# Linear attention and gated experts on one core: weights staged in the maxima's tiles, epsilon on ScalarE, factors transposed straight out of PSUM, another order

## The chip, the cores and the metric

The kernel runs on one core of a Trainium2 chip, in float32 throughout. The metric is device time in microseconds (us). Its engines are TensorE (PE, with its weight loads as PEld), VectorE (DVE), ScalarE (ACT), GpSimd (POOL) and SyncE (SP, which issues the transfers). TensorE writes into PSUM, of which the kernel uses eight banks of 128 partitions x 512 elements; the other engines take the results from there into SBUF.

## What is computed

```python
# q, k, v: [8, 8, 576, 64] (batch, heads, seq, head_dim); w_phi: [64, 128]
def phi(x):
    proj = x @ w_phi
    proj = proj - max(abs(proj), axis=-1)
    return concat([exp(proj), exp(-proj)], axis=-1)
q_p, k_p = phi(q), phi(k)
kv, z = k_p^T v, sum(k_p, axis=seq)
x = (q_p @ kv) / (q_p @ z + 1e-6)            # -> [8, 576, 512]
logits = x @ w_gate                          # 4 experts, the best 2 of each row
w = softmax over the two chosen logits
for e in range(4):
    q, k, v = x @ wq[e], x @ wk[e], x @ wv[e]        # 64 wide
    a = softmax(causal(q k^T / 8)), its sum + 1e-9
    out += w[e] * (a @ v) @ wo[e]
```

## The kernel before

The work is cut into 32 pairs of heads (4 for each of the 8 batches) for the linear attention, and into 16 halves (2 experts each, 2 for each batch) for the experts. Float32 products with weights are made of three products of a high and a low part (`mm`, L302 to L310).

A pair p goes through these steps. `stream_k` (L502) projects the keys; `center` (L544) takes the largest magnitude of each row on VectorE (L550) and subtracts it (L564); ScalarE takes both exponentials (L526, L528, recorded as L321). `stream_kv` (L575) multiplies the key features with v (L591) and with ones (L607), and brings the result into the layout of a stationary operand: for p < KVD = 4 by three transposes on TensorE (L618), for the others by a VectorE transpose (L626) and a way through DRAM, four stores and one load. `stream_q` (L637) projects the queries (L646, recorded as L500), `phi_q` (L661) takes the maximum over partitions on GpSimd (L666), subtracts on VectorE (L668) and takes the exponentials. `stream_n` (L675) computes the denominators (L693) and the numerators (L704).

`fractions` (L709) turns a row of sums into factors laid out as the numerators are. It is called for each pair and, from `sums` (L973), for each half, 48 times in all. VectorE transposes the sums in 32x32 blocks out of PSUM into a tile `wide` (L715); ScalarE picks the 4 x 9 columns that count and writes them back into the same PSUM bank (L720); VectorE adds epsilon (L722) and takes the reciprocal (L723), for the experts also times the gate (L726); one copy spreads the 18 values to 576 columns, each 32 times, into `wide` (L730, on ScalarE or VectorE; recorded as L319 or L331), the bank is released, and VectorE transposes `wide` into `xf` or `rb` (L733). `divide` (L736) multiplies the numerators with `xf` and splits the quotient x into a high and a low part.

A batch then takes `stream_b` (L755): q and k projections (`proj_t`), scores (L825), their evacuation, the mask on GpSimd (L929), `maxima` (L932): the largest of the key blocks in the tile `top` (L939, L942), the maximum over partitions on GpSimd into the tile `max` (L946), subtraction (L950) and exponentials; `sums` (L988) and `attend` (L997, L1017) make y, `evac_y` scales it and splits it, `project_out` (L1040) multiplies both halves' y with wo into eight products (4 tiles of 128 rows, 2 parts of 256 and 320 columns), `evac_o` copies them into one of two tiles `ot`, and `store` writes a tile to DRAM.

The weights arrive in pieces (`split_w`, `split_piece`, L421 to L442): two transfers of 64 partitions into a stage, a rounded copy (high part), and a subtraction (low part). Pieces have up to 576 columns; qk and wo are staged in `ot0`, vg in `ot1`. `load` (L340) issues all transfers from SyncE's queue.

The order of all instructions is made by a planner (`Plan`, L113 to L268) when the kernel is built. Each stream yields a `Step` with its engine or engines, what it needs and what must be done before. The planner keeps a clock per engine and takes, of the steps that could start within WINDOW of the earliest, the one with the lowest rank. A rank is the pair's or batch's number plus the constants POS, POS1, BOFF, SLOPE and MOVE; HOT is taken off for evacuations, OTHER is added for a step on TensorE with another array tiling than the last (128x128 for L310 and L618, 64x128 for L500 and L825, 128x32 for L591, L607, L693, L704, L911, L988 and L1017). FLEX is a handicap for copies that VectorE or ScalarE can do. The engines then follow that order (`in_order`). While nothing else is there at the start, `keep_warm` (L466) issues matmuls on a constant tile.

```python
        st = Step(copies(S), [pk], hot=True)                          # L728
        yield st
        copy(st.eng, S, X.rearrange("p (t i) -> p t i", i=32), both.unsqueeze(2).to_broadcast([128, 18, 32]), [key], [pk])
        plan.release('c', (pk, ps))
        yield Step('DVE', [key], pred=free, hot=True)
        dve(S, wk, [key], 1.1).transpose(out, X)                      # L733
```

Of the kernel before, what the change touches and what calls it, by code (L numbers as in the profile page):

```python
# [21 lines left out]
NJ = 5  # L22
# [18 lines left out]
HOT = 8.54  # L41
SLOPE = (-34.57, 3.93, 4.47, 8.35, -11.91)
UB = 4
SADD = 0
FLEX = (281, -146)
QB = 1
EKB = 2
# [3 lines left out]
WINDOW = 45.0  # L51
SWITCH = 0.0
# [3 lines left out]
ZEROS = 31.82  # L56

MOVE = {
# [29 lines left out]

POS = {'p0': 5.23, 'p1': -38.0, 'v0': 13.08, 'gate': -8.29, 's0': 6.44, 's1': -1.9, 'm0': 9.53, 'm1': 13.64, 't0': -7.83, 't1': 10.17, 'out': 21.57}
NPAIRS = B * NP  # L90
HEAD = 2.4
ADDS = (0, 2)
KVD = 4
RATE = 2.18
TRATE = 2.37
CHANGE = (150.0, 190.0)
PORT = 350.0
OTHER = 6.05
LDW = 109.0
PSUM_TILES = (("c", 8, 512),)  # L100


def moved(x, i):

# [1030 lines left out]
```

## Time and profile before

| | |
|---|---|
| median of 3 runs | 631.66 us (630.19 to 631.81) |
| the profiled execution, its own time | 634.48 us |
| its span, first to last instruction | 632.7 us |
| TensorE matmuls, busy | 615.0 us, 8442 instructions |
| VectorE, busy | 559.3 us, 1176 |
| ScalarE, busy | 444.5 us, 1052 |
| GpSimd, busy | 250.3 us, 167 |
| granted TensorE clock, mean | 0.994 |

The profile is of one execution; times in it are counted from the span's start. Busy times are unions of an engine's instructions. Matmuls overlap in the pipeline, so that the time of one (some 300 ns) is longer than the distance to the next; what a run of them costs is seen in the chain of waits, which follows the work that ended last back from the end, at each step to what released it or to the instruction before it. The kernel's lines L310, L314, L319, L321, L331 and L500 are helpers that several steps share, so that the names of the tiles (out<-in) tell which step it is. A granted clock of 1.00 is 2.4 GHz; the lower level is 1.2 GHz.

### The profile page before, as it was taken

The page shows a single profiled execution, that of the slowest core. Times are in us where ns is not written, and L with a number is a line of the kernel's source. Part 1 is how long each engine was busy: PE and PEld are TensorE (multiplying, and loading weights), DVE is VectorE, ACT ScalarE, POOL GpSimd, SP SyncE. Part 2 cuts the span into 40 slices and gives each one's busy share as a digit, 9 for nine tenths or more (in the row PEclk, how much of TensorE's full clock was granted, in tenths as well). Part 3 has the DMA queues.
Part 4 walks back from the last instruction along what each step waited for, and adds up shares of the span by engine and source line. Part 5 has one row for each costly group of instructions (what it writes and reads, how often), then busy time and mean ns, then how long its engine had stood idle before and what let it go on. Part 6 is the DMA issues. An engine that isn't in the chain of part 4 may idle for free.

```text
span 632.7 us, 20442 instructions
## 1 busy us (share of the span) xinstructions
PE 615.0 (97%) x8442; PEld 479.7 (76%) x8442; DVE 559.3 (88%) x1176; ACT 444.5 (70%) x1052; POOL 250.3 (40%) x167
## 2 busy tenths in 40 slices
PE   8899999999999999999999999999999999999996
PEld 7675688668796778868886878867798578877985
DVE  6599999999998999999999999899967999776782
ACT  3499688568686798676776886676857678664653
POOL 0474626282244544225165506074017254510520
PEclk9899999999999999999999999999999999999998
DMA  6553412341233421234213422142421211110021
GB/s 169 165 153 108 129 48 73 97 116 37 70 115 98 115 66 60 90 102 117 70 51 108 131 89 67 35 142 84 126 94 32 79 48 26 61 43 3 1 76 76
DMA packets 43691, 53.29 MB, mean 84 GB/s; under 512 B 22480, under 2 KB 26576, under 8 KB 43600
## 3 DMA queue, kind: packets, MB, share of 16 engines
q1 hardware_dynamic: 43600, 52.00, 28.5%
q8 instruction: 66, 1.08, 0.7%
q14 instruction: 25, 0.20, 0.1%
HBM read 37.04 MB, written 14.94 MB: 82 GB/s over the span
## 4 chain that ended last, share of the span: by engine, by line
PE 65%; DVE 17%; ACT 8%; issue 3%; POOL 3%; DMA 2%; SPq 1%; DVEq 0%; ACTq 0%; POOLq 0%
PE ps_c L310 27%; PE ps_c L500 8%; PE ps_c L591 7%; PE ps_c L704 6%; PE ps_c L825 5%; PE ps_c L1017 5%; PE ps_c L693 3%; PE ps_c L988 2%; DVE top L942 2%; DVE s L950 2%; DMA ot<-in_wts_dram 2%; ACT u L319 2%; PE ps_c L607 1%; POOL max L946 1%; DVE zs L537 1%
## 5 line engine op out<-in xcount | busy, mean ns | idle before, releaser
L666 POOL PARTITION_ALL_REDUCE mx<-u x64 | 142.8, 2276 | 149.3 <-ACT u L319 146.2
L310 PE MATMUL ps_c<-xh,qk 128*128 128x320 f32 (+1 forms) x512 | 105.7, 297 | 0.0
L929 POOL TENSOR_SCALAR_AFFINE_SELECT s<-s 128x256 f32<-128x256 f32 (+1 forms) x80 | 46.1, 608 | 140.0 <-ACT s L319 123.2
L946 POOL PARTITION_ALL_REDUCE max<-top x16 | 61.8, 3864 | 66.9 <-DVE top L942 53.1
L310 PEld LDWEIGHTS ps_c<-xh,qk 128*128 128x128 f32 x512 | 82.6, 188 | 2.2 <-ACT u L319 0.9
L321 ACT ACTIVATE ek<-ek 128x1152 f32<-128x1152 f32 x64 | 74.9, 1170 | 8.0 <-DVE ek L564 7.2
L310 PE MATMUL ps_c<-xl,qk 128*128 128x256 f32 (+1 forms) x256 | 75.5, 295 | 1.9 <-DVE xl L314 1.9
L591 PE MATMUL ps_c<-ek,v_in 128*32 128x256 f32 x1280 | 75.4, 381 | 0.8 <-ACT ek L321 0.4
L950 DVE TENSOR_TENSOR s<-s,max 128x1152 f32<-128x1152 f32 (+4 forms) x80 | 71.4, 918 | 5.2 <-POOL max L946 5.1
L591 PEld LDWEIGHTS ps_c<-ek,v_in 128*32 128x32 f32 x1280 | 39.8, 110 | 29.6 <-issue 1.6
L321 ACT ACTIVATE s<-s 128x1152 f32<-128x1152 f32 (+4 forms) x80 | 56.5, 743 | 4.8 <-DVE s L950 4.5
L310 PE MATMUL ps_c<-vg,xh 128*128 128x260 f32 (+1 forms) x320 | 59.6, 287 | 0.0
L550 DVE TENSOR_REDUCE pmax<-ps_c 128x4 f32<-128x512 f32 (+1 forms) x96 | 49.4, 539 | 8.6 <-PE ps_c L500 7.2
L319 ACT COPY s<-ps_c 128x512 f32<-128x512 f32 (+4 forms) x141 | 49.3, 448 | 10.8 <-PE ps_c L825 10.8
L668 DVE TENSOR_TENSOR u<-u,mx 128x576 f32<-128x576 f32 x64 | 56.4, 896 | 0.5 <-POOL mx L666 0.5
L310 PE MATMUL ps_c<-yh,wo 128*128 128x256 f32 (+1 forms) x256 | 54.2, 307 | 2.4 <-ACT yh L319 2.4
L321 ACT ACTIVATE mx<-u 128x576 f32<-128x576 f32 x64 | 43.9, 687 | 12.5 <-DVE u L668 12.3
L537 DVE TENSOR_TENSOR zs<-zs,ek 128x512 f32<-128x512 f32 x56 | 51.5, 920 | 0.6
L319 ACT COPY u<-ps_c 128x256 f32<-128x256 f32 (+1 forms) x122 | 41.3, 408 | 14.1 <-PE ps_c L500 14.0
L500 PE MATMUL ps_c<-q_in,wf 64*128 64x320 f32 (+1 forms) x256 | 45.6, 440 | 5.5 <-DMA q_in<-in_qt_dram 2.5
L564 DVE TENSOR_TENSOR ek<-ps_c,pmax 128x512 f32<-128x512 f32 (+1 forms) x96 | 50.0, 536 | 0.0
L310 PEld LDWEIGHTS ps_c<-xl,qk 128*128 128x128 f32 x256 | 48.1, 188 | 2.3 <-DVE xl L314 2.3
(124 smaller groups left out, 1426.8 us busy)
## 6 DMA issues: line engine op xcount, KB each, us to landing
v_in<-in_v_dram SPq DMA_DIRECT2D x32, 320.0 KB, 3.0
q_in<-in_qt_dram SPq DMA_DIRECT2D x64, 144.0 KB, 2.9
out_dram<-ot SPq DMA_DIRECT2D x32, 288.0 KB, 2.1
kvd<-kvt SPq DMA_DIRECT2D x112, 48.0 KB, 1.9
kv<-kvd SPq DMA_DIRECT2D x28, 192.0 KB, 2.4
k_in<-in_kt_dram SPq DMA_DIRECT2D x32, 144.0 KB, 2.8
k_in<-in_kt_dram SPq DMA_DIRECT2D x32, 128.0 KB, 2.7
ot<-in_wts_dram SPq DMA_DIRECT2D x10, 144.0 KB, 3.2
```

Of the source, the lines that this page charges most:

```text
L310: nc.tensor.matmul(o, a, b, start=start, stop=stop, skip_group_check=True)
L319: nc.scalar.copy(o, i)
L321: nc.scalar.activation(o, i, func, **kw)
L500: nc.tensor.matmul(o, a, b, start=True, stop=True, skip_group_check=True)
L537: dve(512, ['zs'], ekk, 1.11, True).tensor_tensor(out=zs, in0=zs if a > 1 else x[:, :, :, 0], in1=x[:, :, :, a], op=ALU.add)
L550: dve(n * 128, [mk], [pk]).tensor_reduce(out=m[:, us], in_=src, axis=AX.X, op=ALU.max, apply_absolute_value=True)
L564: dve(n * 128, [e1k], [pk, mk]).tensor_tensor(out=ek2[p % EKB][:, 1, us, :], in0=src, in1=m[:, us].unsqueeze(2).to_broadcast([128, n, 128] ...
L591: nc.tensor.matmul(o[g, 0:2], v_in[:, 4 * h + t if t < 4 else 8 + h, k:64:2], ek[:, :, u_, :].rearrange("p c (w f) -> p c w f", w=4), star ...
L666: nc.gpsimd.partition_all_reduce(M, U, 128, bass_isa.ReduceOp.absmax)
L668: dve(S, [uk], [mk], port=True).tensor_tensor(out=U, in0=U, in1=M, op=ALU.subtract)
L946: nc.gpsimd.partition_all_reduce(big.rearrange("p e s -> p (e s)"), top.rearrange("p e s -> p (e s)"), 128, bass_isa.ReduceOp.max)
L950: dve(2 * (S - 128 * j), [('d', x, j)], [('max', z)], 1.11, True).tensor_tensor(out=block(s_, j, None, rows(j)), in0=block(s_, j, None, ro ...
```

## The change

- `fractions`: ScalarE's small copies add epsilon as the bias of an activation, the VectorE addition is gone. The spreading copy is gone: VectorE's second transpose reads the 18 values in PSUM with a step of zero, and the bank is released behind it.
- Weights: pieces of up to 1152 columns, staged in `top` and `max` in place of `ot` (qk in both, vg in `top`, wo in `max`, the last two behind all of qk). The first `maxima` waits for vg and wo. Their ranks are constants of their own: 7.17, 21.48 and 24.58.
- The q loads of the first two pairs are issued from ScalarE's queue.
- `project_out`: in the last batch (LAST = 7) the eight products are started when the first half's y is there, one tile's two at once and the others behind `attend` of the second half; each keeps its bank and is finished when the second half's y comes. In other batches a product waits for its own columns of y only.
- KVD is 6: pairs 4 and 5 too go through TensorE's transposes.
- `row` shares the memory of `ge`. KADD, KPOOL and PSUB are switches that, as set (3, 0, 0), leave `key_sum`, the sums of z and `phi_q` as they were.
- The planner's constants: OTHER 6.05 to 12.77, SWITCH 0 to 22, WINDOW 45 to 52, HOT 8.54 to 16.28, FLEX (281, -146) to (447, -293), all of POS, POS1, BOFF, SLOPE and MOVE, and its estimates for a transfer.

```diff
-HOT = 8.54
-SLOPE = (-34.57, 3.93, 4.47, 8.35, -11.91)
+HOT = 16.28
+SLOPE = (-37.28, -27.25, 9.68, 3.86, -6.2)
...
-FLEX = (281, -146)
+LAST = 7
+KADD = 3
+KPOOL = 0
+FLEX = (447, -293)
+PSUB = 0
...
-WINDOW = 45.0
-SWITCH = 0.0
+WINDOW = 52.0
+SWITCH = 22.0
...
-BOFF = (-6.43, -0.31, 4.51, 3.42, -4.56, -1.55, 18.35, 7.14)
+BOFF = (-2.11, 8.18, 6.82, 2.05, 1.07, 6.82, 22.72, -5.5)
...
-KVD = 4
+KVD = 6
...
-OTHER = 6.05
+OTHER = 12.77
...
-    def load(o, i, w, r=()):
-        plan.transfer(o.free_size() * o.partition_size() / 90.0, 475 if o.partition_size() == 128 else 650, [w], list(r))
-        nc.sync.dma_start(o, i)
+    def load(o, i, w, r=(), eng='SP'):
+        n = o.partition_size()
+        plan.transfer(o.free_size() * n / (55.0 if n == 128 else 45.0), 400 if n == 128 else 560, [w], list(r), eng)
+        (nc.scalar if eng == 'ACT' else nc.sync).dma_start(o, i)
...
-        for k, c0 in enumerate(range(0, n, S)):
-            pieces.append((name, c0, min(n, c0 + S), stage[k % len(stage)], src))
+        for k, c0 in enumerate(range(0, n, 2 * S)):
+            pieces.append((name, c0, min(n, c0 + 2 * S), *stage[k], src))
...
-        key, m = st.tensor.name, c1 - c0
-        yield Step('SP', pred=has('w', 1 if name == 'wo' else 0))
-        load(st[0:64, 0:m], src[0:128:2, c0:c1], (key, 0))
+        m = c1 - c0
+        yield Step('SP', pred=has('w', 0 if name == 'qk' else 1))
+        load(st[0:64, 0:m], src[0:128:2, c0:c1], key)
...
-    w_qk = split_w("qk", WQK, [ot[0]], wts[:, WP:c_vg])
-    w_vg = split_w("vg", WVG, [ot[1]], wts[:, c_vg:c_vg + WVG])
-    w_wo = split_w("wo", WO, [ot[0]], wts[:, c_vg + WVG:])
+    stages = [(t[0].rearrange("p e s -> p (e s)"), (n, 0)) for t, n in ((tops, "top"), (maxs, "max"))]
+    w_qk = split_w("qk", WQK, stages, wts[:, WP:c_vg])
+    w_vg = split_w("vg", WVG, stages, wts[:, c_vg:c_vg + WVG])
+    w_wo = split_w("wo", WO, stages[1:], wts[:, c_vg + WVG:])
...
-            yield Step('SP', pred=has('proj_q', p - IB) if p >= IB else None), of_pair('lq', p)
+            eng = 'ACT' if p < IB else 'SP'
+            yield Step(eng, pred=has('proj_q', p - IB) if p >= IB else None), of_pair('lq', p)
...
+                load(q_in[p % IB][64 * h:64 * h + 64, :], qt[p][:, S * h:S * h + S], (f'q_in{p % IB}', h), (), eng)
...
-                act(9, b3[w, :, src], X[r, 0:S // 2:32], [pk], [key])
+                act(9, b3[w, :, src], X[r, 0:S // 2:32], [pk], [key], bias=eps)
         yield Step('DVE', [pk], hot=True)
-        dve(18, [pk], []).tensor_scalar(out=both, in0=both, scalar1=eps, scalar2=None, op0=ALU.add)
         dve(18, [pk], [], 5.0).reciprocal(both, both)
...
-        st = Step(copies(S), [pk], hot=True)
-        yield st
-        copy(st.eng, S, X.rearrange("p (t i) -> p t i", i=32), both.unsqueeze(2).to_broadcast([128, 18, 32]), [key], [pk])
+        yield Step('DVE', [pk], pred=free, hot=True)
+        dve(S, wk, [pk], 1.1).transpose(out.rearrange("p (t i) -> p t i", i=32), both.unsqueeze(2).to_broadcast([128, 18, 32]))
         plan.release('c', (pk, ps))
-        yield Step('DVE', [key], pred=free, hot=True)
-        dve(S, wk, [key], 1.1).transpose(out, X)
...
-        free = lambda: ('m', n, 0) in done and (n < TB or ('max', n - TB) in done)
+        free = lambda: ('m', n, 0) in done and (('max', n - TB) in done if n >= TB else ('w', 2) in done and ('w', 3) in done)
...
-        if g == 1:
+        if g == (b < LAST):
...
-        wwo = wsp["wo"]
         for t in range(4):
-            for s0, s1 in PARTS:
-                yk = [('y' + x, g, s0) for x in "hl" for g in range(2)]
-                pk, ps = yield Step('PE', yk, 'c', lambda: ('w', 3) in done and has_y(2 * b) and has_y(2 * b + 1)), of_batch('out', b) + SLOPE[4] * t / 4
-                n = 0
-                for g in range(2):
-                    wc = slice(512 * g + 128 * t, 512 * g + 128 * t + 128)
-                    for y_, w_ in ((0, 0), (0, 1), (1, 0)):
-                        mm(ps[:, 0:s1 - s0], wwo[w_][:, wc], ys[g][y_][:, s0:s1], n == 0, n == 5, s1 - s0, pk,
-                           yk + [('wo', w_)])
-                        n += 1
-                plan.spawn(evac_o(b, t, s0, s1, pk, ps), of_batch('out', b))
+            for i, (s0, s1) in enumerate(PARTS):
+                if b < LAST:
+                    yield from out_unit(b, t, s0, s1)
+                else:
+                    plan.spawn(out_unit(b, t, s0, s1), of_batch('out', b) + SLOPE[4] * (2 * t + i) / 8)
             plan.spawn(store(b, t), of_batch('out', b))
         done.add(('o', b))
+
+    def out_unit(b, t, s0, s1):
+        wwo = wsp["wo"]
+        n = 0
+        for g in range(2):
+            yk = [('y' + x, g, s0) for x in "hl"]
+            if not g:
+                ks = yk if b >= LAST else [('y' + x, h, s0) for x in "hl" for h in range(2)]
+                pk, ps = yield Step('PE', ks, 'c', lambda: ('w', 3) in done and ('y', 2 * b, s0) in done and (('av', 2 * b + 1) in done or t < 1 if b >= LAST else ('y', 2 * b + 1, s0) in done)), of_batch('out', b) + SLOPE[4] * t / 4
+            elif b >= LAST:
+                yield Step('PE', yk, pred=lambda: ('y', 2 * b + 1, s0) in done), of_batch('fin', b)
+            wc = slice(512 * g + 128 * t, 512 * g + 128 * t + 128)
+            for y_, w_ in ((0, 0), (0, 1), (1, 0)):
+                mm(ps[:, 0:s1 - s0], wwo[w_][:, wc], ys[g][y_][:, s0:s1], n == 0, n == 5, s1 - s0, pk, yk + [('wo', w_)])
+                n += 1
+        plan.spawn(evac_o(b, t, s0, s1, pk, ps), of_batch('out', b))
...
-                     (weights(w_qk, ('w', 1)), 1.5), (weights(w_vg, ('w', 2)), 2.5),
-                     (weights(w_wo, ('w', 3)), 3.5), (stream_kv(), 0), (stream_n(), 0), (stream_s(), 0), (stream_t(), 0)):
+                     (weights(w_qk, ('w', 1)), POS1['wq']), (weights(w_vg, ('w', 2)), POS1['wv']),
+                     (weights(w_wo, ('w', 3)), POS1['wo']), (stream_kv(), 0), (stream_n(), 0), (stream_s(), 0), (stream_t(), 0)):
```

## Rows read from the trace of the kernel before

**Rows 1.** The page's first part: busy us (share of the span) x instructions

```profile
PE 615.0 (97%) x8442; PEld 479.7 (76%) x8442; DVE 559.3 (88%) x1176; ACT 444.5 (70%) x1052; POOL 250.3 (40%) x167
```

**Rows 2.** Busy time by stretch: us, busy (x) per engine, PEclk, DMA share, GB/s

```profile
0.00:5.20 5.20, 3.15 (x30) 2.98 (x30) 2.70 (x27) 0.00 (x0) 0.79 (x7) 1.00 0.38 98
...
19.50:36.00 16.50, 16.48 (x245) 12.06 (x249) 12.11 (x23) 10.40 (x20) 11.07 (x5) 0.90 0.47 132
...
50.00:550.00 500.00, 494.00 (x6779) 381.32 (x6776) 468.87 (x958) 369.64 (x884) 215.15 (x139) 1.00 0.29 83
...
621.00:632.70 11.70, 8.01 (x45) 7.59 (x45) 0.92 (x2) 3.62 (x9) 0.00 (x0) 0.82 0.26 101
```

**Rows 3.** TensorE's waits: line and what ended them, us, times, longest

```profile
PE ps_c L500 <- DMA q_in<-in_qt_dram: 2.5, 1, 2.5
PE ps_c L310 <- ACT yh L319: 2.4, 1, 2.4
PE ps_c L500 <- ACT s L319: 2.0, 2, 1.1
```

**Rows 4.** The chain of waits, its pieces: start us, us, what

```profile
86.09 6.54 PE ps_c L310 x48
92.63 2.08 PE ps_c L704 x32
...
95.68 1.76 PE ps_c L825 x24
97.44 2.30 PE ps_c L591 x40
...
201.92 0.71 PE ps_c L1017 x20
202.62 1.94 PE ps_c L704 x32
204.56 0.97 PE ps_c L693 x16
205.54 2.16 PE ps_c L591 x40
```

**Rows 5.** The timeline of the start: start us, us, engine, line, out<-in, [idle before]

```profile
14.05 2.38 SPq L342 DMA_DIRECT2D q_in<-in_qt_dram  x4
...
29.07 0.55 PE L618 MATMUL ps_c<-ident,kvt 128*128 128x128 f32 x3
```

**Rows 6.** First and last starts of the split of wo and of `top`

```profile
L314 DVE TENSOR_TENSOR wo<-ot,wo x2: 582/660/739, 43.4 to 50.3; 128x576 fp32r<-128x576 f32 x1, 128x448 fp32r<-128x448 f32 x1
...
L319 ACT COPY top<-s x10: 390/406/429, 87.8 to 586.8; 128x256 f32<-128x256 f32 x10
```

**Rows 7.** Groups by form: out<-in x count, busy us, mean ns, idle before

```profile
L733 DVE STREAM_TRANSPOSE xf<-wided 128x576 f32<-128x576 f32 x32 | 24.5, 766 | 1.4 <-ACT wided L319 1.3
...
L319 ACT COPY ps_c<-wided 64x9 f32<-64x9 f32 x128 | 22.0, 172 | 9.4 <-DVE wided L715 5.7
...
L319 ACT COPY wided<-ps_c 128x576 f32<-128x576 f32 x30 | 19.0, 635 | 9.9 <-DVE ps_c L723 8.6 <-DVE gc L331 1.3
...
L626 DVE STREAM_TRANSPOSE kvt<-ps_c 128x384 f32<-128x384 f32 x28 | 15.9, 567 | 0.4 <-PE ps_c L607 0.2
...
L722 DVE TENSOR_SCALAR ps_c<-ps_c 128x18 f32<-128x18 f32 x48 | 8.3, 173 | 2.1 <-ACT ps_c L319 1.9
...
L321 ACT ACTIVATE gt<-gt 128x20 f32<-128x20 f32 x8 | 1.7, 216 | 8.8 <-DVE gt L893 8.8
...
L331 DVE COPY wided<-ps_c 128x576 f32<-128x576 f32 x2 | 1.5, 751 | 0.0
```

**Rows 8.** The chain of waits at the end: start us, us, what

```profile
621.04 8.03 PE ps_c L310 x45
...
629.14 0.43 ACT ot L319
```

**Rows 9.** DMA issues: KB each, median us from issue to landing

```profile
out_dram<-ot SPq DMA_DIRECT2D x32, 288.0 KB, 2.1
```

More of the change, by code (lines that the diff above doesn't have):

```diff
@@ L55 @@
 PHASE = 0.0
[L56 removed]
+ZEROS = 25.27
 MOVE = {
[10 rows of a table removed]
[L69 to L75 removed]
[6 rows of a table removed]
[L82 to L85 removed]
@@ new lines @@
+    'gate': (21.06, -7.98, 0.45, 5.93, 7.7, 21.37, -4.48, -0.04,),
+    't1': (2.39, -6.96, 9.54, 2.66, 2.78, -2.05, -16.41, -10.56,),
+    'out': (2.04, 0.98, -0.33, 1.86, -5.09, 8.46, 7.73, -5.97,),
+    'fin': (0, 0, 0, 0, 0, 0, 0, 0.22,),
+}
+POS1 = {'wq': 7.17, 'wv': 21.48, 'wo': 24.58, 'n0': -30.0, 'n1': 2.78, 'k': -0.6, 'q': -13.78, 'v': -0.62, 'kv': -23.5, 'z': 3.8, 'cen': -4.87, 'evu': -35.73, 'ph0': 17.23, 'ph1': 17.65, 'div': -1.88, 'evd': -4.7, 'lk': -16.22, 'lq': 24.67}
+BOFF = (-2.11, 8.18, 6.82, 2.05, 1.07, 6.82, 22.72, -5.5)
@@ L90 @@
+POS = {'fin': 39.8, 'p0': -3.53, 'p1': -40.28, 'v0': 21.78, 'gate': -24.77, 's0': -7.94, 's1': -10.44, 'm0': 9.16, 'm1': 14.32, 't0': -27.77, 't1': 0.1, 'out': 21.12}
 NPAIRS = B * NP
-HEAD = 2.4
+HEAD = 2.48
 ADDS = (0, 2)
-KVD = 4
+KVD = 6
 RATE = 2.18
@@ L187, in run, with transfer @@
             self.ready[k] = self.last[k] = (end, eng)
-    def transfer(self, cost, issue, w, r):
-        t = self.free['SP']
+    def transfer(self, cost, issue, w, r, eng='SP'):
+        t = self.free[eng]
         for k in r:
-            t = max(t, self.after(self.ready, k, 'SP'))
+            t = max(t, self.after(self.ready, k, eng))
         for k in w:
-            t = max(t, self.after(self.last, k, 'SP'))
-        self.free['SP'] = t + issue
+            t = max(t, self.after(self.last, k, eng))
+        self.free[eng] = t + issue
         self.rings = max(self.rings, t + issue + 650.0) + cost
@@ L534, in key_sum @@
         x = ek[:, :, 0:8, :].rearrange("p c (h a) f -> p c h a f", h=2)
-        for a in range(1, 4):
+        for a in range(1, 4 if KADD == 3 else 1):
             yield Step('DVE', ekk, pred=has('kv', p - 1) if p else None, port=True)
             dve(512, ['zs'], ekk, 1.11, True).tensor_tensor(out=zs, in0=zs if a > 1 else x[:, :, :, 0], in1=x[:, :, :, a], op=ALU.add)
+        for c in range(0 if KADD == 3 else 2):
+            st = Step((('POOL', KPOOL), ('DVE', 65 + 1.11 * 512)) if KPOOL else 'DVE', ekk, pred=has('kv', p - 1) if p else None, port=True)
+            yield st
+            plan.run(st.eng, KPOOL if st.eng == 'POOL' else 65 + 1.11 * 512, ['zs'], ekk, port=st.eng == 'DVE')
+            (nc.gpsimd if st.eng == 'POOL' else nc.vector).tensor_tensor(out=zs[:, c], in0=x[:, c, :, 0:2], in1=x[:, c, :, 2:4], op=ALU.add)
         for h in range(0 if TAILPE else 2):
@@ L595, in stream_kv @@
                 yield Step('PE', ['zs'], pred=has('zs', p), hot=True, slack=LATE[1], tiling=(128, 32))
-            for t in range(1 + TAILPE if adds else NJ):
+            first = 1 if KADD == 3 else 2
+            for t in range(first + TAILPE if adds else NJ):
                 for h in range(2):
@@ L599, in stream_kv @@
                         g = 64 * h + 32 * c
-                        if adds and t == 0:
-                            a_, x_, r_ = ones, zs[:, c, h], ['zs']
+                        if adds and t < first:
+                            a_, x_, r_ = ones, zs[:, c, h] if first == 1 else zs[:, c, h, t], ['zs']
                         elif not adds and t < 4:
@@ L606, in stream_kv @@
                         plan.run('PE', 55, [kc], r_, tiling=(128, 32))
-                        nc.tensor.matmul(o[g:g + 32, 2], a_, x_.rearrange("p (w f) -> p w f", w=4), start=t == 0, stop=t == (4, TAILPE)[adds > 0], skip_group_check=True)
+                        nc.tensor.matmul(o[g:g + 32, 2], a_, x_.rearrange("p (w f) -> p w f", w=4), start=t == 0, stop=t == (first - 1 + TAILPE if adds else 4), skip_group_check=True)
             done.add(('kv', p))
@@ L666, in phi_q @@
         nc.gpsimd.partition_all_reduce(M, U, 128, bass_isa.ReduceOp.absmax)
-        yield Step('DVE', [mk])
-        dve(S, [uk], [mk], port=True).tensor_tensor(out=U, in0=U, in1=M, op=ALU.subtract)
+        st = Step((('POOL', PSUB), ('DVE', 65 + 1.04 * S)), [mk], port=True) if PSUB else Step('DVE', [mk], port=True)
+        yield st
+        plan.run(st.eng, PSUB if st.eng == 'POOL' else 65 + 1.04 * S, [uk], [mk], port=st.eng == 'DVE')
+        (nc.gpsimd if st.eng == 'POOL' else nc.vector).tensor_tensor(out=U, in0=U, in1=M, op=ALU.subtract)
         yield Step('ACT', [uk])
```

33 lines of the change are left out of this document (14 added, 19 removed), and 32 rows, old and new, of the table MOVE.

## The prediction

> **What bounds it now.** I read the busy times of the page first: TensorE is busy 97% of the span, and no other engine is near it over the whole [rows 1]. A busy TensorE may still hide waits, so I read three views behind it. The windows show what it does by stage [rows 2]: in the 500 us from 50 to 550 it idles 6.0 us (500 less 494.00), while VectorE is busy 468.87 of them. So TensorE is the bound, VectorE the one that mostly feeds it, ScalarE (369.64) has room. The list of TensorE's waits names the big ones [rows 3]: 2.5 us for the first q tile, 2.4 us for the last `yh`, 2.0 us for ScalarE's copies of scores. The warm-up matmuls on a constant tile count as busy and are no work. The chain of waits, cut into pieces, gives the price of dense work [rows 4]: 48 projection matmuls in 6.54 us, 136 ns each.
>
> The same rows hold a cost that no wait shows. The 32 matmuls of L704 take 2.08 us behind L310 but 1.94 us behind L1017, which is tiled like them, the 40 of L591 take 2.30 us behind L825 and 2.16 us behind L693. So a change between the three array tilings (128x128, 64x128, 128x32) costs 0.14 us. From the run of L310 at 86.09 us to that of L591 at 97.44 there are three changes (to L704, L825 and L591), one in 3.8 us; over 632.7 us that makes 167, or 23 us. What can be had in all is thus the idle time, the warm-up, those 23 us, and time at the lower clock level: the granted clock is 0.90 from 19.5 to 36 us and 0.82 from 621 on [rows 2], so part of each stretch runs at 1.2 GHz instead of 2.4, both times behind one of the two long waits. About 1.6 us (0.10 x 16.5) and 2.1 us (0.18 x 11.7) of full-speed work are lost there.
>
> **The base.** Durations come from the profiled execution: 634.48 us, span 632.7, so 1.8 lie around the span. The median of the runs is 631.66, 2.8 below it; I sum differences and put them on the median.
>
> **Start: -4.0.** The first q tile is issued behind weight pieces on SP's queue, at 14.05 us [rows 5], and TensorE waits 2.5 us for it. The change issues the q loads of pairs 0 and 1 from ScalarE's queue, which does nothing in the first 5.2 us [rows 2]; four issues there delay nothing. The wait goes (-2.5), and with it most of the slow clock behind it (1.6). What is late next is the first key features' chain (projection, VectorE, exp), for which the warm-up fills in; two q projections that come earlier take the place of some of it. I take -4.0; bounds 0 (another load is as late) and -8 (as much again, where real matmuls take the place of the warm-up's).
>
> **Weights: 0.** Eight pieces of up to 576 columns become four of up to 1152, half the instructions for the same bytes and elements; the staging moves from `ot` to `top` and `max`, and the steps get a later rank (7.17, 21.48, 24.58 against 1.5 to 3.5). The first maxima now wait for the split of vg and wo. Today the last subtraction of wo starts at 50.3 us and the first `top` is written at 87.8 us [rows 6], so 37 us cover it. If that cover goes, see the rivals. Behind a weight piece on SP stand the next pairs' k, q and v.
>
> **Factors, 48 times (32 pairs, 16 halves).** Away go the addition of epsilon (173 ns of VectorE each, 8.3 us) and the spreading copy (46 on ScalarE at 635 ns, 29 us: the 30 shown for the pairs and 16 like them for the halves; two on VectorE at 751, 1.5 us) [rows 7]. The big transpose now reads PSUM with a step of zero. No row shows that operation, so I bound it: the transpose of 576 out of SBUF takes 766 ns, the one of 384 out of PSUM 567; they lie on one line of 1.04 ns an element, so the source costs nothing, and VectorE's copy out of PSUM with the same zero step (751) shows the step costs nothing either. I take 766; the upper bound is 766 + 751 = 1517 (the copy's work comes back), which gives 36 us of VectorE. The Trainium skill speaks against this part (VectorE: DVE Perf Modes, section "The TRN2 errata"): a PSUM source costs VectorE 62 cycles more than an SBUF one, 65 ns at its 0.96 GHz; by that estimate 3.1 us in 48, which would leave 6.7 of the 9.8 us saved. The transposes on one line do not bear it out.
>
> Epsilon as a bias of ScalarE's 192 small copies: 172 ns now; the nearest row for an activation this short is 216, so 0 to 44 ns each, 0 to 8.4 us in all, on an engine that idles 130 of the 500 us in the middle; I take 0 on the path. The Trainium skill (ScalarE: Activation LUTs, section "What ACT_TABLE_LOAD costs") adds about 93 ns if the bias is a pointer operand; by that estimate it is 18 us of ScalarE, and still not on TensorE's path. No row of this trace shows a copy with a bias.
>
> So VectorE loses 9.8 us, ScalarE some 25, and the chain from a sum to its factor shortens by 635 + 173 ns and their hops, about 1 us. The larger handicap on VectorE's copies (281 to 447 ns) shifts further copies to ScalarE. TensorE gains in the middle only what it idles there, 6.0 us at most: a third, **-2.0**. Bounds -5 and +18: the PSUM bank is now held through the transpose, see the rivals.
>
> **Order: -2.3.** The rank penalty for changing the tiling doubles (6.05 to 12.77) and a candidate that changes it counts 22 ns later; but the ranks that it competes with have about doubled too. I take a tenth of the 23 us; bounds +3 and -6.
>
> **Two more pairs through TensorE's transposes: +1.1.** Pairs 4 and 5 leave the way through DRAM (its four stores and a load each) and take three transposes, 0.55 us [rows 5], with their two changes of tiling partly shared.
>
> **Tail: -4.4.** Now the first piece of the last y is ready at 621.04 and 45 output matmuls follow in 8.03 us; the last copy starts at 629.14 and takes 0.43 [rows 8]; from 621.04 to the end of the span are 11.7. First, copy, epsilon and hops leave the chain ahead of it: -1.0. Second, for the last batch the half of each output product that comes from the first two experts is computed ahead, in banks held open, while TensorE would sit idle; 24 matmuls remain behind the last y, 3.3 us at full clock. But the 4.7 us won on TensorE can't all be had: the two `ot` buffers are next. An output tile takes six matmuls (0.8 us) and a copy of 0.4, so tile 0 is complete at +1.2 and, at 2.1 us from issue to landing [rows 9], stored by 3.4; tile 1's store lands by 4.2; tile 3 can be copied only then, two copies, so by 5.1, and lands by 7.2. The closing that now follows the last landing (632.7 - 629.57 - 2.1 = 1.0) makes it 8.3 against 11.7: -3.4.
>
> **Sum.** -4.0 - 2.0 - 2.3 + 1.1 - 4.4 = -11.6: 634.48 becomes 622.9, the median 631.66 becomes 620.1, say **620**.
>
> **Rivals.** (a) *Only the ends move.* The relief of VectorE is on an engine that TensorE seldom waits for, and the order changes as many tilings as before: -4.0 - 4.4 + 1.1 = -7.3, 624.4. For it: 494 of 500 us busy. Against it: VectorE at 94% in the middle is the likeliest cause why the order has to break up runs of one tiling. 0.22. (b) *More order.* With VectorE eased the middle loses most waits (-5) and a quarter of the changes (-5.8): -4.0 - 5 - 5.8 + 1.1 - 4.4 = -18.1, 613.6. 0.17. (c) *Slower, by banks.* There are eight PSUM banks, and TensorE already waits for ScalarE's evacuation of one [rows 3]. In each of 48 divisions the bank is kept 0.77 us longer, more if VectorE is behind or `xf` isn't free. If 15 of the 48 show up on TensorE (11.6 us), the gain is gone; at 24 (18.5 us) it is 631.66 - 11.6 + 18.5 = 638.6. Against it: the planner counts the bank as held and orders around it. 0.08. (d) *Weights too late.* The maxima's first use is pushed behind the split of wo. TensorE has the next batch's pairs to go on with, so only a delay well beyond the 37 us of cover costs; it takes 11.6 us of bare waiting to undo the change, 631.7, the same as before. 0.06.
>
> **Numbers.** Forecast 0.47, with 615 to 625 for its own terms. A measurement of this kernel tells 0.3% (1.9 us) from no change. Faster: 0.47 + 0.22 + 0.17 = 0.86; same 0.06; slower 0.08. The range runs from 611, just under (b), to 631, just under (d), and leaves (c), (d) and some of (b)'s lower side out.
>
> **What would show it.** Start: no wait for q in TensorE's list, first q projections before 10 us, granted clock 1.0 up to 36. Factors: the rows of L722 and of the copies to `wide` gone, 48 transposes out of PSUM near 766 ns; VectorE's busy time near 540 to 548. Order: pieces of the chain with longer runs of one tiling. Tail: at most 24 output matmuls behind the last y, waits of the last copies for stores of `ot`, about 8 us from the last y to the end. It would be wrong if the transposes took over 1 us, if TensorE's waits for ScalarE or VectorE's release of a bank grew beyond 6 us in the middle, or if the first `top` came far behind 88 us with TensorE idle before it.

## The result, and the profile after

The changed kernel takes 620.99 us (median of 4 runs, 619.75 to 622.08) against 631.73 for the kernel before (630.19 to 633.12): a ratio of 0.983, with an interval of 0.980 to 0.986. That is 10.7 us less, where 11.6 were forecast. Its profiled execution took 620.78 us, with a span of 619.0; the one before had a span of 632.7, and its own time stood 2.8 us above its median. So the two traces differ by 13.7 us, three more than the medians, and the readings below are of the traces. Of 39 further executions of the kernel before, the nine with a mean granted clock of 0.999 or more took 631.3 us in the median and the six with 0.995 or less 634.3; the profiled one had 0.994, so its trace holds more time at the lower clock level than most. In the later groups of runs the kernel before has medians of 632.3 to 632.7 us, and two variants that time like the changed kernel (620.99 and 621.2 us, below) stand 11.3 and 11.5 us under it.

The first part of the page (busy time, share of the span, instructions), and the first line of its chain of waits:

```profile
PE 607.7 (98%) x8391; PEld 477.7 (77%) x8391; DVE 541.4 (87%) x1115; ACT 424.2 (69%) x1011; POOL 246.0 (40%) x167
...
PE 77%; DVE 11%; ACT 9%; issue 1%; DMA 1%; ACTq 0%; DVEq 0%
```

Against [rows 1], VectorE has 17.9 us less and ScalarE 20.3 less, yet TensorE is still the bound. Its own 7.3 us less are no work taken off it: 3.3 are warm-up matmuls, and about 3 are matmuls that ran at the lower clock level before (1.6 at the start, 1.5 in the tail, both below). The rest of the gain is that it stands less. The stretches (us; busy time and instructions of PE, PEld, DVE, ACT, POOL; granted clock, DMA share, GB/s):

```profile
19.50:36.00 16.50, 16.50 (x273) 10.49 (x266) 13.92 (x25) 16.11 (x37) 11.74 (x6) 1.00 0.76 205
...
50.00:550.00 500.00, 496.72 (x6817) 390.60 (x6810) 454.21 (x916) 351.70 (x839) 206.09 (x136) 1.00 0.28 82
...
607.00:619.00 12.00, 7.04 (x70) 6.20 (x62) 3.03 (x7) 3.07 (x8) 0.00 (x0) 0.89 0.25 98
```

A finer cut of the end:

```profile
616.00:619.00 3.00, 0.00 (x0) 0.00 (x0) 0.00 (x0) 0.00 (x0) 0.00 (x0) 0.58 0.43 167
```

Beside [rows 2]: the clock from 19.5 to 36 us is 1.00 instead of 0.90. The 0.89 of the last stretch costs nothing: the clock is low only behind the last matmul (0.58 from 616 us on). In the 500 us of the middle TensorE idles 3.3 us instead of 6.0, and it got through more: 6817 matmuls instead of 6779. TensorE's waits (line and what ended them; us, times, longest):

```profile
PE ps_c L509 <- DMA q_in<-in_qt_dram: 1.1, 1, 1.1
PE ps_c L315 <- DVE col L356: 1.0, 1, 1.0
PE ps_c L315 <- DVE xl L319: 1.0, 1, 1.0
PE ps_c L605 <- ACT ek L326: 0.9, 1, 0.9
```

The three long waits of [rows 3] are gone: nothing waits for the last `yh`, and ScalarE's copies of scores show up with 0.2 at a time. The 1.1 us for q is not what is left of the 2.5. It stands at 5.2 us, before TensorE's first projection, where the kernel before waited as long for its first k:

```profile
PE ps_c L500 <- DMA k_in<-in_kt_dram: 1.1, 1, 1.1
```

All listed waits came to 13.9 us before and come to 6.1 now. The rows of the factors and of the small copies with epsilon as bias (count | busy us, mean ns):

```profile
L745 DVE STREAM_TRANSPOSE xf<-ps_c 128x576 f32<-128x576 f32 x32 | 24.5, 765 | 0.1
...
L326 ACT ACTIVATE ps_c<-wided 64x9 f32<-64x9 f32 x128 | 23.5, 183 | 9.7 <-DVE wided L732 6.0
```

The transpose out of PSUM with a step of zero takes 765 ns; I had taken 766 [rows 7]. The copy went from 172 to 183 ns: 2.1 us more of ScalarE in 192.

**Where the 13.7 us went.** I laid the matmuls of both traces in the order of their starts, left the warm-up out, and compared the moments at which TensorE had done equal work. The changed kernel is about 6 us ahead at 50 us, 9 to 10 at 290 and 11.5 at 601; its last matmul starts 15.0 us earlier, and its span ends 13.7 earlier. That makes about 6 from the start, 5.5 from the middle and 2.2 from the tail. Since the two orders differ, such readings move by 1 to 2 us with the place and with what is counted (matmuls or their columns). The sum of the forecast was right; this division was not.

### The profile page after: what moved, and what is told of

Read it like the earlier page. It is cut to its first block, busy times and chain, and to the rows that moved or that the text cites. A ratio compares the mean times of both kernels' runs of the same rounds, so it can differ in the third digit from the quotient of the medians.

```text
span 619.0 us, 20200 instructions
## 1 busy us (share of the span) xinstructions
PE 607.7 (98%) x8391; PEld 477.7 (77%) x8391; DVE 541.4 (87%) x1115; ACT 424.2 (69%) x1011; POOL 246.0 (40%) x167
## 4 chain that ended last, share of the span: by engine, by line
PE 77%; DVE 11%; ACT 9%; issue 1%; DMA 1%; ACTq 0%; DVEq 0%
PE ps_c L315 32%; PE ps_c L605 9%; PE ps_c L509 9%; PE ps_c L721 7%; PE ps_c L1030 6%; PE ps_c L838 5%; PE ps_c L1001 3%; PE ps_c L710 3%; PE ps_c L622 2%; DVE zs L546 2%; ACT ek L326 2%; ACT u L324 2%; ACT mx L326 1%; DVE u L685 1%; DVE top L955 1%
## 5 line engine op out<-in xcount | busy, mean ns | idle before, releaser
L315 PE MATMUL ps_c<-xh,qk 128*128 128x320 f32 (+1 forms) x512 | 106.5, 299 | 1.8 <-DVE xl L319 1.0
L315 PEld LDWEIGHTS ps_c<-xh,qk 128*128 128x128 f32 x512 | 82.8, 188 | 4.4 <-DVE xl L319 1.2
L959 POOL PARTITION_ALL_REDUCE max<-top x16 | 58.8, 3676 | 67.8 <-DVE top L955 61.3
L942 POOL TENSOR_SCALAR_AFFINE_SELECT s<-s 128x256 f32<-128x256 f32 (+1 forms) x80 | 44.4, 590 | 89.8 <-ACT s L324 89.4
L315 PE MATMUL ps_c<-xl,qk 128*128 128x256 f32 (+1 forms) x256 | 75.6, 295 | 0.0
L963 DVE TENSOR_TENSOR s<-s,max 128x1152 f32<-128x1152 f32 (+4 forms) x80 | 68.2, 880 | 4.9 <-POOL max L959 4.9
L685 DVE TENSOR_TENSOR u<-u,mx 128x576 f32<-128x576 f32 x64 | 60.9, 959 | 2.2 <-POOL mx L681 2.2
L315 PE MATMUL ps_c<-vg,xh 128*128 128x260 f32 (+1 forms) x320 | 59.0, 285 | 0.2 <-ACT s L324 0.2
L324 ACT COPY s<-ps_c 128x512 f32<-128x512 f32 (+4 forms) x136 | 48.0, 460 | 8.9 <-PE ps_c L838 8.9
L315 PE MATMUL ps_c<-yh,wo 128*128 128x320 f32 (+1 forms) x256 | 52.8, 301 | 0.0
L324 ACT COPY u<-ps_c 128x320 f32<-128x320 f32 (+1 forms) x126 | 41.3, 411 | 15.6 <-PE ps_c L509 15.3
L315 PEld LDWEIGHTS ps_c<-vg,xh 128*128 128x128 f32 (+1 forms) x320 | 47.5, 177 | 1.3 <-ACT s L324 0.5
L315 PEld LDWEIGHTS ps_c<-xl,qk 128*128 128x128 f32 x256 | 48.2, 188 | 0.0
L509 PEld LDWEIGHTS ps_c<-wf,k_in 64*128 64x128 f32 x576 | 41.7, 191 | 8.0 <-DVE u L336 1.0
```

The costliest lines, as they stand in the source:

```text
L315: nc.tensor.matmul(o, a, b, start=start, stop=stop, skip_group_check=True)
L324: nc.scalar.copy(o, i)
L509: nc.tensor.matmul(o, a, b, start=True, stop=True, skip_group_check=True)
L685: (nc.gpsimd if st.eng == 'POOL' else nc.vector).tensor_tensor(out=U, in0=U, in1=M, op=ALU.subtract)
L942: nc.gpsimd.affine_select(out=d, in_=d, pattern=[[0, 2], [1, w]], compare_op=ALU.is_ge, fill=FILL, base=0, channel_multiplier=-1)
L959: nc.gpsimd.partition_all_reduce(big.rearrange("p e s -> p (e s)"), top.rearrange("p e s -> p (e s)"), 128, bass_isa.ReduceOp.max)
```

## The experiments

Of the twelve runs below, ten keep the order of every engine's instructions but for what their edit names (a transfer, a copy, an addition, the last products), so that little but the edited thing can move the time. Two let the planner order everything anew. Each was timed beside the kernel before, whose medians in the three groups of runs were 632.5, 632.7 and 632.3 us.

### The tail without the split

```diff
-LAST = 7
+LAST = 8
```

> The changed kernel with LAST = 8, so that the last batch's output products too start only when both halves' y are there; the order is the same up to them. Theory (computing the first half ahead is worth what the prediction gave it, 3.4 us): 624 us, and 48 output matmuls behind the last y instead of 30. Rival (the wait for the two output tiles gives it back): within 0.5 us of 621.

Measured: 620.93 us (620.34 to 621.37), ratio 0.9816 [0.9797, 0.9836], the same as the changed kernel. The split gains nothing. The ends of the two chains of waits show why. First the changed kernel (start us, us, what):

```profile
608.06 4.40 PE ps_c L315 x30
...
612.48 0.44 ACT ot L324
...
612.93 2.10 DMA out_dram<-ot
...
615.21 0.49 DVE ot L336
```

TensorE's last matmul ends at 614.0, but the end of the span hangs on a store: the copy at 615.21 waited until the buffer `ot` had been stored. Without the split:

```profile
608.28 0.38 ACT yh L324
...
608.70 6.50 PE ps_c L315 x45
...
615.28 0.49 DVE ot L336
```

Here 45 matmuls follow the last y, and the last copy starts at 615.28, 0.07 us later. What the split takes from behind the last y is waited out at `ot`. It is less than planned, too: without the split TensorE stands only 0.8 us for the last `yh`.

### Four output buffers, with and without the split

In the last batch the first two `q_in` tiles, by then without a reader, serve as the third and fourth output buffer:

```diff
+    def outs(b, t):
+        return (q_in[t - 2], f'q_in{t - 2}') if b >= LAST and t > 1 else (ot[t % 2], f'ot{t % 2}')
...
-        o, ok = ot[t % 2], ('ot', t % 2, s0)
+        o, ok = outs(b, t)[0], (outs(b, t)[1], s0)
...
```

> The changed kernel, with four output buffers instead of two in the last batch (the first two q_in tiles, free by then, serve as the third and fourth). Order of TensorE the same; two last copies go from VectorE to ScalarE. Theory: the end is set by the two output buffers, whose copies wait for stores. Then the last copies follow the last matmul (614.0) at once: 614.0 + 0.9 (two copies in a row) + 2.1 (store) + 1.2 (closing) = 618.2 of span instead of 619.0, or 617.8 with one copy of 0.45: 619.8 to 620.5 for the median. Rival: the last matmuls themselves, or the closing, set the end: 621 within 0.3, and the copies' waits for stores are gone without the span getting shorter.

Measured: 619.41 us (618.79 to 620.63), ratio 0.9791 [0.9770, 0.9812], span 617.6: a little under the theory's 619.8 to 620.5. Then the same with the last product unsplit (`LAST = 8`, the buffers as above):

> The changed kernel with four output buffers in the last batch and without the split of the last product (all of its output matmuls follow the last y). Theory: the split gains only where the buffers don't bind: the last matmul comes 1.2 to 1.6 us later than with the split and four buffers (613.9), and the copy and the store follow at once: 620.6 to 621.1 against 619.4. Rival: the split is worth nothing in either case: 619.1 to 619.8. The prediction's 3.4 would make it 622.8.

Measured: 620.58 us (619.22 to 621.18), ratio 0.9807 [0.9780, 0.9834], span 619.4. The ends of both chains, first with the split:

```profile
604.08 0.99 PE ps_c L315 x6
605.07 2.84 PE ps_c L1030 x56
607.91 6.02 PE ps_c L315 x42
...
613.95 0.43 ACT q_in L324
```

```profile
608.81 0.38 ACT yh L324
...
609.23 6.52 PE ps_c L315 x45
...
615.78 0.42 ACT q_in L324
```

With four buffers the last copy follows the last matmul at once in both, and 3.2 us later (617.6 less 614.38, 619.4 less 616.20) the span is over. So two buffers cost 1.6 us of median (1.8 against the 621.2 of the same group of runs, below), and once they don't bind, the split is worth 1.2: its chain runs through TensorE alone, without a gap, while the unsplit one passes through y, and TensorE stands 0.8 us for `yh` in front of L315. The 1.2 are at the edge of the noise (618.79 to 620.63 with the split, 619.22 to 621.18 without), and the two stem from different groups of runs. The first rows also show how little the split computes ahead: 6 of the 24 matmuls come before the last product with v (L1030), the other 18 behind it, in one run with the 24 that need the last y. The variant with four buffers and the split has the lowest median of all runs, 1.6 us under the changed kernel and 13.3 under the kernel before. Its interval overlaps that of the changed kernel (0.980 to 0.986), but the spans and the chains say the same as the medians.

### The factors alone, in the order of before

```diff
-                act(9, b3[w, :, src], X[r, 0:S // 2:32], [pk], [key])
+                act(9, b3[w, :, src], X[r, 0:S // 2:32], [pk], [key], bias=eps)
...
-        dve(18, [pk], []).tensor_scalar(out=both, in0=both, scalar1=eps, scalar2=None, op0=ALU.add)
+        dve(18, [pk], [])
...
+        nc.vector.transpose(out.rearrange("p (t i) -> p t i", i=32), both.unsqueeze(2).to_broadcast([128, 18, 32]))
```

(The spreading copy and the old transpose go; `xf` and the factors of the halves get one more buffer each, so that the order can stay.)

> The kernel before with the new factors alone: epsilon as a bias on ScalarE, no spreading copy, the transpose straight out of PSUM with a step of zero (into one more buffer of xf and of rb, so that the banks are released where they were). TensorE's, GpSimd's and SyncE's orders are those of before, instruction by instruction. Theory (TensorE is the bound, it wins what it idles for VectorE and 1 us at the end): 631.7 falls to 628 to 630. Rival (VectorE is a second bound, 9.8 us less of it count nearly in full): 622 to 625. Third (hidden work): 631 to 632.

Measured: 626.65 us (625.13 to 628.56), ratio 0.9905 [0.9882, 0.9927]: 5.9 us, more than the theory's 2 to 4 and less than the rival's 7 to 10. TensorE's longest waits:

```profile
PE ps_c L502 <- ACT s L319: 1.8, 2, 1.1
PE ps_c L310 <- ACT yh L319: 1.2, 1, 1.2
PE ps_c L502 <- DMA q_in<-in_qt_dram: 1.2, 1, 1.2
```

```profile
19.50:36.00 16.50, 16.40 (x258) 11.33 (x258) 14.34 (x23) 11.46 (x22) 13.16 (x6) 1.00 0.50 145
```

Of the three in [rows 3], `yh` and q are waited for half as long, and the granted clock behind both stays at 1.00 (it was 0.90 and 0.82, [rows 2]). At equal work this run, whose matmuls come in the order of before, is 0.8 us ahead of the kernel before at 75 us, 4.3 at 600 and 6.9 at the end. The middle thus gains 3.5, in steps spread over the whole stretch, and the tail 2.6: 1.1 up to the output matmuls, and 1.5 in them, because they run at full clock.

### The old factors, and epsilon alone, in the new order

```diff
-                act(9, b3[w, :, src], X[r, 0:S // 2:32], [pk], [key], bias=eps)
...
+                nc.scalar.copy(b3[w, :, src], X[r, 0:S // 2:32])
...
+        nc.vector.tensor_scalar(out=both, in0=both, scalar1=eps, scalar2=None, op0=ALU.add)
         dve(18, [pk], [], 5.0).reciprocal(both, both)
...
-        dve(S, wk, [pk], 1.1).transpose(out.rearrange("p (t i) -> p t i", i=32), both.unsqueeze(2).to_broadcast([128, 18, 32]))
+        nc.scalar.copy(X.rearrange("p (t i) -> p t i", i=32), both.unsqueeze(2).to_broadcast([128, 18, 32]))
+        dve(S, wk, [pk], 1.1).transpose(out, X)
```

> The changed kernel with the old factors put back: VectorE adds epsilon, ScalarE copies the 576 columns into the tile, VectorE transposes from there; TensorE's, GpSimd's and SyncE's orders are those of the changed kernel. Theory: 2 to 4 us longer (623 to 625), 1 of it at the end. Rival (the new order leaves no room for 8.3 us more of VectorE and 29 us more of ScalarE): 629 or more. Third: under 1 us.

Measured: 641.96 us (640.94 to 643.7), ratio 1.015 [1.0129, 1.0172]: 21 us above the changed kernel, and slower than the kernel before. VectorE's waits in this run:

```profile
DVE xf L748 <- ACT wided L747: 18.3, 27, 1.6
...
DVE rb L748 <- ACT widey L747: 8.1, 12, 1.3
```

That is the rival's 629 or more. In the changed order nothing stands on VectorE between the spreading copy and the transpose, so VectorE waits 26.4 us for ScalarE's copies, and hands the delay on: TensorE's listed waits come to 20.0 us instead of 6.1, none over 1.3. To part the copy from the additions, a second run brought back the additions (and the copies without a bias) alone:

> The changed kernel with epsilon added by VectorE again (48 additions, 173 ns each, 8.3 us) and ScalarE's 192 small copies without a bias; the transposes out of PSUM with a step of zero stay, all orders the same. Theory: of the 21 us that the old factors cost in this order, most came from VectorE's waiting for ScalarE's spreading copy in the middle of a division; the additions alone cost a third to a half of their own time: 623.5 to 626. Rival: VectorE is so full in this order that all its time comes through: 628 or more.

Measured: 623.77 us (622.98 to 624.25), ratio 0.9858 [0.9828, 0.9887].

```profile
L740 DVE TENSOR_SCALAR ps_c<-ps_c 128x18 f32<-128x18 f32 x48 | 8.3, 173 | 1.9 <-ACT ps_c L738 1.7
```

So 8.3 us of VectorE cost 2.8 us, a third, and, if the two add up, the copy the other 18 of the 21; the copy alone was not run. It brings two things, the hop from VectorE to ScalarE and back, and more work on ScalarE (446.6 us busy instead of 424.2). No run parts them; that VectorE waits 26.4 us for it speaks for the hop. And the 18 us hold for an order laid without the copy: where copy and additions had their place in the order, taking both away gave 5.9 us (the factors alone).

### Either structure with the other's order

The planner's constants (ranks, penalties, per-step offsets) changed hands. The changed code with the constants of before:

> The changed kernel's code (new factors, four weight pieces, six pairs through TensorE's transposes, split last product, q loads of pairs 0 and 1 on ScalarE's queue), ordered by the planner with the constants of the kernel before; the weights have ranks 1.5, 2.5 and 3.5. Theory: the factors alone gave 5.9 us of the 10.7; what is left needs the new order, so this run stands at 625 to 628. Rival: the new code brings all of it and the order nothing: 620 to 622.5. Second rival: the old constants only fit the old code: 631 or more.

Measured: 661.61 us (660.28 to 662.83), ratio 1.0456 [1.0433, 1.048]. And the code of before with the changed constants:

> The kernel before's code (epsilon added by VectorE, spreading copy, eight weight pieces, no split at the end, four pairs through TensorE's transposes), ordered by the planner with the constants of the changed kernel. Theory: the new order only pays where the factors leave VectorE and ScalarE room; with the old factors it is slower than the kernel before: 633 to 645, with TensorE's waits for VectorE and ScalarE over 14 us in all. Rival: the order's gain (fewer tiling changes, start) is its own and adds to that of the factors: 626 to 629.

Measured: 661.73 us (656.33 to 662.8), ratio 1.0447 [1.0417, 1.0478]. Both are slower than either kernel, by 29 to 41 us. The first is the second rival's "631 or more", by much; the second lies beyond the theory's 645. The waits and three stretches of the first run (columns as above):

```profile
PE ps_c L1000 <- ACT s L325: 14.8, 4, 11.8
```

```profile
126.00:140.00 14.00, 6.16 (x84) 4.32 (x76) 13.26 (x22) 9.71 (x17) 14.00 (x7) 0.89 0.54 160
140.00:150.00 10.00, 3.35 (x40) 1.30 (x40) 10.00 (x11) 5.42 (x9) 6.76 (x3) 0.50 0.00 0
150.00:160.00 10.00, 7.62 (x90) 4.35 (x94) 4.93 (x11) 6.41 (x17) 0.00 (x0) 0.62 0.01 2
```

and those of the second:

```profile
PE ps_c L698 <- ACT mx L326: 12.1, 2, 11.5
```

```profile
75.00:80.00 5.00, 3.51 (x32) 1.53 (x36) 0.48 (x1) 4.03 (x10) 0.00 (x0) 0.50 0.00 0
```

In each, one wait of over 11 us stands out, while the engines that feed TensorE are at work (VectorE 13.3 and GpSimd all of the 14 us before 140 us in the first); behind it the granted clock is 0.50, the 1.2 GHz level, and the matmuls that then run are slow too. At equal work the first run falls about 20 us behind the changed kernel there, and the second about 13 behind the kernel before; the rest is lost in later steps. These two runs therefore don't measure "the order alone": they show that constants found for one code don't carry over to another, and that the mismatch costs more than all that the change gained. The order's own share has to be read otherwise (below).

### The start

The kernel before, with the q loads of pairs 0 and 1 issued at once from ScalarE's queue:

```diff
...
+    for p in range(IB):
+        for h in range(2):
+            nc.scalar.dma_start(q_in[p][64 * h:64 * h + 64, :], qt[p][:, S * h:S * h + S])
     plan.loop()
```

> The kernel before with the q loads of the first two pairs issued from ScalarE's queue at the very start; all other orders as before. Theory (the wait of 2.5 us and the low clock behind it go): 631.7 falls by 2.5 to 4, to 628 to 629. Rival (another load is as late, or the warm-up takes the place of the wait): less than 1 us.

Measured: 634.33 us (631.68 to 636.42), ratio 1.0028 [1.0012, 1.0044]: no gain, but 1.8 us more. What is late next is k:

```profile
PE ps_c L503 <- DMA k_in<-in_kt_dram: 3.0, 1, 3.0
```

That wait was 1.1 us before, and behind it the warm-up matmuls run slowly. The same 81 in this run and, below, before:

```profile
9.84 6.24 PE L310 MATMUL ps_c<-warm 128*128 128x128 bf16 x81
```

```profile
6.62 4.70 PE L310 MATMUL ps_c<-warm 128*128 128x128 bf16 x81
```

At equal work this run is 4.8 us behind the kernel before at the second k (11 us), level at 25 us, as the wait for q and the slow clock behind it are gone, and 1.7 behind from 60 us on. So what the forecast gave to the early q does come, and the long wait with its slow stretch has moved to k. The DMA share of the first 5.2 us is 0.59 instead of 0.38 [rows 2]: the q transfers share it with the first k, which the old order of TensorE wants first. In the changed order TensorE starts with q. The changed kernel with q issued from SP, ahead of each pair's k:

```diff
-        (nc.scalar if eng == 'ACT' else nc.sync).dma_start(o, i)
+        nc.sync.dma_start(o, i)
```

> The changed kernel with the four q loads of pairs 0 and 1 issued from SyncE instead of ScalarE; they stand between wf and the k pieces there, all other orders the same. Theory: what matters is that the weight pieces come late, not which queue issues q: the k pieces are issued about 1.2 us later each (two issues ahead of each pair's), and the warm-up covers it: 620.5 to 622. Rival: the second queue is what lets k and q arrive together, and the start loses 2 to 4 us: 623 to 625.

Measured: 621.2 us (619.76 to 621.31), ratio 0.9813 [0.9792, 0.9834]: the same. Then the first two weight pieces where the kernel before had its first ones (`ahead` issues the two transfers of that piece; the planner's bookings are unchanged):

```diff
+            if p in (1, 2):
+                ahead(p - 1)
             done.add(('load_k', p))
```

> The changed kernel with the loads of its first two weight pieces issued on SP where the kernel before issued its first ones: the first piece (two transfers) ahead of the first two v loads, the second behind the third k load; q stays early on ScalarE's queue, all orders of the engines are the same. Theory: late weights are what brings k, v and q in time, so their 590 KB ahead of v (about 3 us at the 199 GB/s of this stretch) come back as a wait of TensorE: 622.5 to 625. Rival: the loads are not what made the start shorter but the order in which TensorE uses them: 621 within 0.7.

Measured: 620.99 us (619.58 to 621.75), ratio 0.9811 [0.9783, 0.9839]: the same, against my theory. And, with that, the four q loads on SP behind the first piece:

> As the run before, and the q loads of pairs 0 and 1 issued on SP behind the first weight piece, as the kernel before had them; all orders of the engines are those of the changed kernel. Theory: the first q tile lands several us later, TensorE stands and its clock falls, as before: 4 to 6 us, 625 to 627. Rival: the warm-up covers it and the start's gain is the order's: 621 to 623.

Measured: 627.59 us (626.61 to 628.34), ratio 0.9918 [0.9891, 0.9946]: 6.6 us slower, a little more than the theory's 4 to 6.

```profile
PE ps_c L527 <- DMA q_in<-in_qt_dram: 7.1, 1, 7.1
```

```profile
5.20:19.50 14.30, 8.26 (x95) 7.40 (x96) 4.48 (x8) 3.81 (x10) 5.36 (x3) 0.76 0.70 195
```

TensorE stands 7.1 us for q, the clock is 0.76 in the stretch, and the 5.9 us by which this run is behind at 15 us are still 5.8 at the end. So the queue doesn't matter, nor the weights' place by itself: what pays is q in time *and* an order that begins with it. The changed kernel's first q projections (start us, us; the idle time before in brackets):

```profile
5.18 2.29 PE L509 MATMUL ps_c<-q_in,wf 64*128 64x256 f32 x8 [1.08 <-DMA q_in<-in_qt_dram]
...
10.23 4.36 PE L315 MATMUL ps_c<-warm 128*128 128x128 bf16 x75
```

They stand where the kernel before ran warm-up. The tile `warm` in all, after and before (count: min/median/max ns, first and last start):

```profile
L315 PE MATMUL ps_c<-warm x117: 219/219/314, 1.0 to 43.2; 128*128 128x128 bf16 x117
```

```profile
L310 PE MATMUL ps_c<-warm x174: 218/219/315, 1.0 to 52.2; 128*128 128x128 bf16 x174
```

57 fewer, at 58 ns each (4.36 us for 75), are 3.3 us.

## Why the prediction was right, and where its steps were not

The forecast of 620 stands against 621.0, and its main case was the right one: TensorE stayed the bound, and the gain came from its waits, the warm-up and the clock. That the sum came out so near is in part luck, as errors of its terms cancel. Term by term, in us of the traces:

| term | predicted | measured |
|---|---|---|
| start | -4.0 | about -6 |
| factors, middle | -2.0 | -3.5 (order of before) |
| order (tiling changes) | -2.3 | -2.7 by count, not isolated |
| two more pairs through TensorE | +1.1 | not tried alone |
| tail: chain | -1.0 | -1.1 (order of before) |
| tail: split | -3.4 | 0.0 (-1.2 with four buffers); the slow clock counted in it: -1.5, without the split |

**Start: mechanism half right, size short.** The wait of 2.5 us for q went, and so did the slow clock behind it (1.6). "What is late next ... for which the warm-up fills in" left out that real projections would now take the place of 57 warm-up matmuls, 3.3 us, which I had only allowed as the far bound. Against that, TensorE now stands 0.95 us between 36 and 50 us, where it stood 0.05; its idle time in the first 50 us fell from 5.1 to 3.1 us in all. That makes 2.0 + 1.6 + 3.3 = 6.9, against about 6 read from the traces. I had also put it down to ScalarE's queue; the runs show that the queue is irrelevant, and that the early load without the changed order only moves the long wait to k.

**Weights: 0 was right.** The first `top` is written at 77.7 us (87.8 before, [rows 6]), and their loads' place moved nothing.

```profile
L336 DVE COPY top<-s x4: 251/378/490, 77.7 to 586.8; 128x256 f32<-128x256 f32 x4
```

**Factors: price right, worth too small.** The transpose cost what I took. The reading behind it was weak: two points always lie on one line. A third transpose out of PSUM, of 288 elements in the kernel before, bears it out, as the line of 1.04 ns an element gives 467 ns there:

```profile
L715 DVE STREAM_TRANSPOSE wided<-ps_c 128x288 f32<-128x288 f32 x32 | 15.1, 471 | 1.0 <-PE ps_c L693 0.8
```

By the Trainium skill (VectorE: DVE Perf Modes, section "The TRN2 errata") a PSUM source costs VectorE 62 cycles more than an SBUF one, which would make the transpose, as an estimate, 831 ns. The trace has 765 and doesn't bear it out here. The 93 ns that the Trainium skill (ScalarE: Activation LUTs, section "What ACT_TABLE_LOAD costs") gives for a pointer operand didn't come up: the kernel hands epsilon over as a number, and the row shows 11 ns more.

The step that failed is "a third" of the 6.0 us that TensorE idled in the middle. It was 3.5 us of lead on an unchanged order. In the tail the chain's 1.0 was right (1.1), and the factors alone also won the 1.5 us of slow clock, which I had counted in the split's term. How VectorE's relief becomes TensorE's time in the middle is argued, not shown: the run with the additions converts VectorE's time to the kernel's at a third, in the changed order, and 9.8 us less of it at that rate would be 3.3.

**Order.** Between matmuls in the order of their starts, the warm-up left out, I count 176 changes of tiling before and 157 after; 19 at the 0.14 us of [rows 4] are 2.7 us, where I took 17 (2.3). With the warm-up the counts are 188 and 163, but those six more lie in the first 52 us and belong to the start. Factors and order together, less the 1.1 for two more pairs, make 5.1 for the middle, against 5.5 read. That is a sum that closes, not a proof: neither the tiling changes nor the two pairs were tried alone, since any edit to either makes the planner order everything anew, and the runs with exchanged constants show what that does.

**Tail: the split fell.** I had seen that the two `ot` buffers would bind, and cut the gain to 3.4 for it. The step that failed is "while TensorE would sit idle". TensorE hardly sits idle there (0.8 us for `yh` without the split, where the kernel before stood 2.4), and of the 24 matmuls only 6 ran ahead of the last product with v. The other 18 follow it in one run with the last 24, so that the last y is no longer the start of the last chain, and the `ot` waits come on top. From the first piece of the last y (about 608.3) to the end it is 10.7 us, where I had 8.3. And the price of the old way was overrated: its 8.03 us for 45 matmuls [rows 8] held slow clock, and with the clock at full speed the same 45 take 6.50.

So terms were missed on both sides: the start, the factors in the middle, the order and the tail's chain were too small by 2.0, 1.5, 0.4 and 0.1, the split's term, with the clock in it, too large by 1.9. Mended, they make -13.7, as the two traces differ; with readings good to 1 or 2 us, that they meet so well proves nothing. The medians differ by 10.7, as the profiled execution of before stood 2.8 above its median with more time at the lower clock level, so the forecast of 11.6 met the medians better than its terms met the traces. Rival (b) had the right direction for the middle, (a) was wrong in holding VectorE's relief for worthless (the factors alone gave 5.9 us). Of (c), the banks, and (d), the weights, nothing shows: no wait of the middle is longer than 1.0 us.

## What to carry to other kernels

Before crediting a load that is issued earlier, look at what the bounding engine does first when it lands: early q gained nothing in the old order, 6.6 us in the new one. A copy that makes a chain hop to another engine and back can cost far more than its share of an engine's time, where the order leaves no room for it: put back into the new order, the copy that a step of zero had replaced cost some 18 us, the additions 3, while in the old order, which had a place for both, they had cost 5.9 together. At the end of a kernel, count the output buffers before shortening the matmuls ahead of them, and take the price of the old tail at the clock that the new one will have.

## What was not expected

With the order kept and one operation changed the kernel moved by 0 to 21 us; planned anew with the other kernel's constants it lost 29 to 41, about half of it behind a single wait of over 11 us, after which the granted clock stood at 0.50 in the next stretch. A wait half as long for q (1.2 instead of 2.5 us, the factors alone) left the clock at 1.00 up to 36 us, where the longer one had 0.90; over its six executions that run has mean granted clocks of 0.999 and 1.000, while of the 39 of the kernel before only nine reach 0.999. And the early q, for all that it brought back the 2.5 us and the clock, made the old kernel slower.
